# Attention and a leaky-ReLU layer pair in one kernel: the block loads of the later queries issued by GpSimd instead of SyncE

## The chip, the cores and the metric

The kernel runs on one core of a Trainium2 chip. The core has five engines that each work through their own instructions in order: TensorE (PE in the profile; PEld is its weight load), VectorE (DVE), ScalarE (ACT), GpSimd (POOL) and SyncE (SP, which here only issues transfers). They wait for one another through semaphores. Transfers between the main memory and the on-chip memory are carried out by 16 DMA engines, whichever engine issued them. The metric is the time of one execution in microseconds (us); lower is better.

## The reference, cut to what matters

```python
# q, k, v: (4, 8, 768, 64)   lam: (8,)   w_in: (512, 2048)   w_out: (2048, 512)
for b in range(nb):                       # 12 blocks of 64 positions
    sl = slice(b * block, (b + 1) * block)
    qb, kb, vb = (q[:, :, sl], k[:, :, sl], v[:, :, sl])
    intra = np.einsum('bhic,bhjc->bhij', qb, kb) * Dmask[None]
    intra = np.einsum('bhij,bhjd->bhid', intra, vb)
    inter = np.einsum('bhid,bhde->bhie', qb * lam_pow[None], kv_state)
    out[:, :, sl] = intra + inter
    kb_dec = kb * rev_pow[None]
    kv_state = lam_block[None, :, None, None] * kv_state + np.einsum('bhsd,bhse->bhde', kb_dec, vb)
# out, as x: (3072, 512)
h = x @ w_in
g = np.maximum(0.01 * h, h)
return g @ w_out
```

A decayed linear attention over blocks of 64 positions, with a state per head that each block hands to the next, and then two matrix products with a leaky ReLU between them. All data are float32.

## The kernel before, in words

**Stages.** The 3072 tokens are cut into 24 chunks of 128 (two blocks of 64; 6 chunks for each of the 4 batches). Chunk by chunk the attention is computed (`round_of`), 4 chunks make a group of 512 tokens, and each group goes through the first matrix product against 8 blocks of `w_in` (`up`, TensorE at L709). Every float32 factor is split into three parts (`xh`, `xl`, `xm` and `wh`, `wl`, `wm`), so each product is three passes. The results `g` (buffers `gs`) are stored in main memory (L738, L744) or first combined into sums for a Strassen scheme and then stored (`sums`, L766 and L774). While that goes on, the weights `w_out` are loaded (L578), converted by ScalarE and VectorE (L596 to L603) and stored again (L663). The second product (L834) begins at about 330 us and reads the stored blocks back (L808).

**A round of attention.** For chunk c the scores are computed from the transposed keys `kT` and queries `qT` (64x64 matrix instructions, L321), VectorE applies the decay (L460) and adds to the state (L467), GpSimd scales the state by its decay (L470), the keys (L427) and the queries (L431, which makes `qsT`). `kT`, `qT` and `qsT` have two buffers each.

**Where the transposed queries come from.** Up to chunk 9, chunks are loaded straight (L346) and transposed on TensorE (L411). From chunk `DV = 10` on, the loads deliver the queries and keys cut in blocks of 32x32 and VectorE transposes those (`turn`, L391). `load_subs` (L382) issues these block loads for a run of up to 3 chunks at once: 16 transfers for the keys and 16 for the queries of each run, runs being chunks 10 to 11, 12 to 14, 15 to 17, 18 to 20 and 21 to 23. One transfer fills 32 partitions with 8 (first run) or 12 pieces of 32 numbers each, 32 or 48 KB. The queries land in `kqv_f[1]` (a part of `att`), for the run 12 to 14 in `w32` and `lows`; the keys in the `raws` buffers. Each run's queries must land in a buffer that the run before has been transposed out of. `turn(c)` waits for the loads of its run; what it writes, `kT` and `qT` of chunk c, is read by the scores of that chunk and by L431.

**What sets the order.** No scheduler of the language decides: `Plan` collects every step with its engine, an estimated length, what it reads and writes, and a rank, simulates the engines, and emits the instructions of all engines in the order it found. Steps on `"DMA"` are issued on SyncE; `move` adds such a step, with a length for the issue and a `slack` by which the plan moves back the time at which a consumer may count on the data. `Plan.LAG` holds the delay from an engine's end to its consumer's start (0.12 for POOL, 3.5 for DMA). A changed length or engine of one step therefore changes the order on every engine.

**SyncE's queue.** It holds all transfers of the kernel but one: block loads, chunk loads, weight loads, stores of `g`, of the sums and of the weights. It works in order, so a transfer that waits or takes long holds those behind it.

Of the kernel before, what the change touches and what calls it, by code (L numbers as in the profile page):

```python
# [31 lines left out]
def _bc(ap, idx, n):  # L32
    a = [list(x) for x in ap.ap]
    return bass.AP(ap.tensor, ap.offset, a[:idx] + [[0, n]] + a[idx:])


class Plan:
# [23 lines left out]
    def add(self, eng, us, fn, reads=(), writes=(), rank=0.0):  # L61

        n, deps = len(self.ops), set()
        for k in reads:
            w, r = self.last.setdefault(k, [None, []])
            if w is not None:
                deps.add(w)
            r.append(n)
        for k in writes:
            w, r = self.last.setdefault(k, [None, []])  # L70
            if w is not None:
                deps.add(w)
            deps.update(r)
            self.last[k] = [n, []]
        deps.discard(n)
        ways = {eng: us} if isinstance(eng, str) else dict(zip(eng, us))
        if self.slack:
            self.more[n] = self.slack
        if self.chain is not None:
            self.chains[self.chain].append(n)  # L80
        self.ops.append((ways, fn, deps, (self.rank + rank, n), set(writes)))
# [81 lines left out]
def kernel(  # L163
# [10 lines left out]
    nc = tc.nc  # L174
# [19 lines left out]
    SLACK, GSLACK = 4.0, 2.0  # L194
# [5 lines left out]
    LEAD = 8.0  # L200
    WSLACK = 5.0
    DV = 10
    RUNS = {10: (-8.0, 0.8), 12: (4.0, 0.0)}
    C4 = P // 4
    HALF = (slice(0, D), slice(D, 2 * D))
# [72 lines left out]
    plan = Plan()  # L278
    plan.idle, plan.spare, plan.warm = busy, "b10", 1.3 + 0.22 * WARM
    add = plan.add  # L280
    steady = False

    def length(us, issue=0.5):

        return issue if steady else us

    def move(us, fn, reads, writes, issue=0.5, rank=0.0, slack=SLACK):

        plan.slack = slack if steady else EARLY_SLACK
        if steady and not rank:  # L290
            rank = FIRST
        add("DMA", length(us, issue), fn, reads, writes, rank=rank)
        plan.slack = 0.0


    def factors_k():
        for i in range(2):
            nc.vector.tensor_copy(lam_h[:, i * HP:(i + 1) * HP], lam_b[:, i::2])
        nc.vector.tensor_tensor(eye, ident[:, 0:C2], ident[:, C2:C], op=ALU.add)
        for hi in range(2):  # L300
            for hp in range(HP):
                nc.vector.tensor_tensor_scan(decay[:, hi, hp, :], _bc(lam_h[:, 2 * hp + hi], 1, C2), eye, 0.0,
                                             op0=ALU.mult, op1=ALU.add)
# [9 lines left out]
    lam_c = pow_q[:, :, C2 - 1]  # L313
    plan.rank = -1.0
    add("DVE", 1.95, factors_k, [], ["fk", "sc"])
    add("DVE", 1.25, factors_q, [], ["fq"])
    ENG = {"ACT": nc.scalar, "DVE": nc.vector, "POOL": nc.gpsimd}
# [16 lines left out]
    def of(c):  # L334
        return c // NCB, c % NCB, c % 2
# [3 lines left out]
    def load_kq(c):  # L339
        b, n, i = of(c)  # L340
        for src, x, nm in ((k, 0, "k"), (q, 1, "q")):
            y, dst = src[b, :, n * C:(n + 1) * C, :], kqv[x][i]

            def go(y=y, dst=dst):
                for z in range(2):
                    nc.sync.dma_start(out=dst[:, z * HP:(z + 1) * HP, :], in_=y[z::2].rearrange("h p d -> p h d"))  # L346
            if nm == "k" or c < DV:
                move(1.15, go, [], [f"{nm}{i}"], issue=1.0)

    def run(c):  # L350

        lo = max(DV, c - c % TURN)
        return lo, c - c % TURN + TURN - lo

    def subs(first, n):


        n = n * C
        def rows(x, lo, hi):
            return x[:, :(hi - lo) * n].rearrange("p (y t) -> p y t", t=n), lo, hi  # L360
        ks = [(*rows(raw[-2], 0, 2), [f"raw{NRAW - 2}"]), (*rows(raw[-1], 2, 4), [f"raw{NRAW - 1}"])]
        qs = [(*rows(kqv_f[1], 0, HP), ["q0", "q1"])]

        if first == DV:
            ks = [(*rows(raw[0], 0, HP), ["raw0"])]
        elif first < DV + TURN:
            qs = [(*rows(w32f, 0, 2), ["w320", "w321"])] + [
                (*rows(lows[i].bitcast(F32), 2 + i, 3 + i), [f"low{i}"]) for i in range(2)]
        return ks, qs

    def load_subs(c):
        b, n, i = of(c)
        count = run(c)[1]
        for nm, src, pieces in zip("kq", (k, q), subs(c, count)):
            for sub, lo, hi, keys in pieces:
                add("POOL", 0.0, lambda: None, [], keys, rank=-30.0)
                for y in range(lo, hi):
                    for a in range(4):
                        h = y // 2 + (2 * y + a // 2) % HP * 2
                        z = src[b, h, n * C:(n + count) * C, a % 2 * C4:(a % 2 + 1) * C4]  # L380
                        o = sub[a * C4:(a + 1) * C4, y - lo, :]
                        move(0.55, lambda o=o, z=z: nc.sync.dma_start(  # L382
                                out=o.rearrange("j (m i) -> j m i", i=C4), in_=z.rearrange("(m j) i -> j m i", j=C4)),
                            keys, [f"{nm}s{y}{a}"], issue=SUBL, rank=RUNS.get(c, (4.0, 0.4))[0] + RUNS.get(c, (4.0, 0.4))[1] * (4 * y + a))

# [13 lines left out]
    def transposes(c):  # L399
# [9 lines left out]
        def go(src, at):  # L409
            for y in range(HP):  # L410
                nc.tensor.transpose(out=at[y], in_=src[:, 2 * y:2 * y + 2, :].rearrange("p a d -> p (a d)"), identity=ident)  # L411

        if c < DV:
            add("PE", 0.44, lambda: go(tk, at), [f"k{i}"], [key])
            add("PE", 0.44, lambda: go(tq, [pt[:, y, :] for y in range(HP)]), [f"q{i}"], ["pt"])

        def copies():
            kT = kTs[i]
            into = kT if c < GC else kT.rearrange("p (t a) x -> p t (a x)", t=2)
            src = z if c < GC else z.rearrange("p t a x -> p t (a x)")  # L420
            if c < DV:
                add("ACT", 0.6, lambda: nc.scalar.copy(into, src), [key], [f"kT{i}"])
# [115 lines left out]
    def round_of(c):  # L538

        after = []  # L540
        if c + 2 < NCH:
            load_kq(c + 2)
        plan.begin(c)

        if c < 2 * GC:
            after.append(transposes(c + 2))
        after.insert(0, outputs(c, lambda: after.append(scores(c + 1)) if c + 1 < NCH else None))
        if 2 * GC <= c < NCH - 2:
            after.append(transposes(c + 2))
        plan.end()  # L550
        for x in after:
            x()
        if DV < c + 3 < NCH:
            turn(c + 3)
        if DV + TURN < c + 4 < NCH and (c + 4) % TURN == 0:
            load_subs(c + 4)
        if c + 2 < NCH:
            load_v(c + 2)
# [413 lines left out]
    for n, x in enumerate(seq):  # L972
        plan.rank = float(n)
        steady = begin <= n and x[0] in ("r", "up", "wo")
        if x[0] in "abr":
            {"a": alone, "b": begun, "r": round_of}[x[0]](x[1])
        elif x[0] == "ls":
            load_subs(DV)
            turn(DV)
        elif x[0] == "lt":  # L980
            load_subs(sum(run(DV)))
        elif x[0] == "wi":
            w_in(x[1])
        elif x[0] == "up":
            up(*x[1:])
        elif x[0] == "wo":
            w_out(*x[1:])
        elif x[0] == "wp":
            if not freed:
                add("DVE", 0.0, lambda: None, [], ["psc", "po", "X0", "X1", "Z0", "Z1"])  # L990
                freed = True
            w_out_parts(x[1])
        elif x[0] == "ws":
            if x[1] == 0:
                add("DVE", 0.0, free_attention, [], ATT + [f"e{z}{p}" for z in "hlm" for p in range(NS)])
            w_sums(x[1])
        elif x[0] == "fr":
            add("ACT", 0.0, free_raws, [], [f"raw{i}" for i in range(NRAW)] + ["rh4", "rl4", "rm4", "zr"])
        elif x[0] == "s":
            strassen(*x[1:], LEAD)  # L1000
        elif x[0] == "n":
            plain(*x[1:], LEAD)
        elif x[0] == "copy":
            copy_banks(*x[1:])
        elif x[0] == "add":
            add_banks(*x[1:])
        else:
            plain(*x[1:4], LEAD, True, x[4])
# [31 lines left out]
```

## Time and profile before

| | |
|---|---|
| median of 3 runs | 611.8 us (609.57, 611.80, 612.82) |
| profiled execution, its own time | 613.76 us |
| its span, first to last instruction | 611.9 us |
| granted TensorE clock, mean | 0.99 |
| GpSimd busy, 72 to 275 us | 45.40 of 203 us, 48 instructions |
| VectorE busy, 140 to 280 us | 64.34 of 140 us |
| DMA engines busy, 140 to 280 us | 0.87 |
| packets under 512 bytes, 140 to 280 us | 58413 of 74066 |
| L382, block loads of keys / queries | 80 / 80 issues on SyncE, 94.2 to 272.2 us / 72.8 to 274.6 us |
| one such issue, least / median / most | keys 312 / 490 / 1921 ns; queries into `att` 419 / 474 / 1827 ns |
| from issue to landing, queries, median | 3.1 us (the 48 of 48 KB into `att`) |

The profile is that of one execution. "Busy" counts the time in which an engine carries out instructions; issuing a transfer does not count. A wait is put down to the event that came last: "[2.37 <-ACT b L727]" behind an instruction says that its engine stood 2.37 us before it, until ScalarE's instruction of line 727 had written a tile `b`. "SPq" is SyncE's queue: its rows show when a transfer was issued and how long the issue took, not when the data landed. The granted clock is the share of full speed that TensorE was given.

### The profile page before, as it was taken

The numbers are of one execution on the slowest core, as the hardware profiler recorded it, in microseconds if no ns is written. First come the engines' busy times: TensorE is split into PE (matmuls) and PEld (weight loads), VectorE is DVE, ScalarE is ACT, GpSimd is POOL, SyncE is SP. The second block draws the span as 40 slices with busy tenths as digits, with TensorE's granted clock in tenths as the row PEclk, the third lists the DMA queues.
The fourth block names the chain that finished last, engine by engine and source line by source line (L and its number), as shares of the span: only waits on it lengthen the run. The fifth ranks groups of instructions, "written<-read, shape, count | busy, mean of one in ns | idle before, by whom it ended". The sixth has DMA issues, their size and how long they took to land.

```text
span 611.9 us, 13190 instructions
## 1 busy us (share of the span) xinstructions
PE 591.6 (97%) x5340; PEld 488.7 (80%) x5340; DVE 387.4 (63%) x534; ACT 290.4 (47%) x458; POOL 85.9 (14%) x90
## 2 busy tenths in 40 slices
PE   7899999999989999999999999999999999999994
PEld 6688888888868877888888888888887888878883
DVE  4899764335436327426589849975688695778831
ACT  4678974445545545565576743432334223251300
POOL 1564422114214003203100000000000000000000
PEclk9899999999989999999999999999999999999998
DMA  9899776767889887999889735436465465474433
GB/s 217 212 261 254 228 193 145 171 151 204 196 218 264 216 220 218 235 235 260 265 256 333 233 113 197 170 123 185 139 182 195 152 193 176 155 225 140 158 80 69
DMA packets 190188, 119.88 MB, mean 196 GB/s; under 512 B 128944, under 2 KB 168112, under 8 KB 190128
## 3 DMA queue, kind: packets, MB, share of 16 engines
q1 hardware_dynamic: 189984, 119.05, 68.8%
q8 instruction: 42, 0.69, 0.5%
q14 instruction: 18, 0.15, 0.1%
q10 hardware_dynamic: 144, 0.00, 0.0%
HBM read 79.17 MB, written 39.85 MB: 194 GB/s over the span
## 4 chain that ended last, share of the span: by engine, by line
PE 84%; DMA 4%; SPq 4%; DVE 3%; ACT 2%; issue 1%; DVEq 0%; ACTq 0%
PE b L709 40%; PE b L834 11%; PE psc L834 11%; PE po L834 10%; PE po L321 4%; PE psc L321 4%; PE pt L834 4%; SPq L382 2%; SPq L911 2%; DMA att<-in_v_dram 1%; DMA raws<-in_moe_w_out_dram 1%; DVE xl L814 1%; PE pt L411 1%; DMA xm<-g 1%; DMA raws<-g 1%
## 5 line engine op out<-in xcount | busy, mean ns | idle before, releaser
L709 PE MATMUL b<-xm,wm 128*128 128x512 f32 (+2 forms) x392 | 103.9, 392 | 2.4 <-ACT b L727 2.4
L709 PE MATMUL b<-xh,wh 128*128 128x512 f32 (+2 forms) x392 | 103.5, 387 | 2.3 <-ACT gs L732 1.5
L709 PE MATMUL b<-xl,wl 128*128 128x512 f32 (+2 forms) x392 | 104.4, 390 | 0.0
L709 PEld LDWEIGHTS b<-xh,wh 128*128 128x128 f32 x392 | 72.8, 188 | 18.2 <-ACT gs L732 2.4
L811 ACT ACTIVATE xh<-xm 128x1024 fp32r<-128x1024 f32 x45 | 47.7, 1060 | 81.8 <-DMA xm<-g 50.9
L709 PEld LDWEIGHTS b<-xm,wm 128*128 128x128 f32 x392 | 71.4, 188 | 17.8 <-ACT b L727 3.2
L709 PEld LDWEIGHTS b<-xl,wl 128*128 128x128 f32 x392 | 72.8, 188 | 15.1 <-DVE wl L614 0.3
L732 ACT ACTIVATE gs<-b 128x512 f32<-128x512 f32 (+2 forms) x97 | 56.9, 591 | 50.6 <-PE b L709 37.4
L727 ACT ACTIVATE b<-b 128x512 f32<-128x512 f32 (+2 forms) x97 | 56.1, 581 | 52.2 <-PE b L709 52.0
L814 DVE SCALAR_TENSOR_TENSOR xl<-xm,xh 128x1024 fp32r<-128x1024 f32 x45 | 54.8, 1217 | 28.3 <-ACT xh L811 22.1
L818 DVE SCALAR_TENSOR_TENSOR xm<-xl,xh 128x1024 fp32r<-128x1024 f32 x48 | 58.7, 1225 | 3.5
L470 POOL TENSOR_TENSOR att<-att 128x256 f32<-128x256 f32 x40 | 34.1, 853 | 53.9 <-DVE att L467 53.9
L602 DVE TENSOR_SCALAR w<-w 128x512 int32<-128x512 int32 x32 | 17.6, 550 | 36.9 <-ACT w L596 36.8
L431 POOL TENSOR_TENSOR att<-att 128x512 f32<-128x512 f32 (+1 forms) x20 | 25.2, 1261 | 102.0 <-DVE att L391 53.9
L460 DVE TENSOR_TENSOR att<-psc,att 128x512 f32<-128x512 f32 x24 | 16.5, 689 | 31.3 <-PE psc L321 31.2
L321 PEld LDWEIGHTS po<-att 64*64 64x64 f32 x1472 | 28.3, 140 | 9.1 <-issue 6.0
L321 PE MATMUL po<-att 64*64 64x64 f32 x1472 | 34.1, 228 | 0.6 <-ACT att L499 0.3
L427 POOL TENSOR_TENSOR att<-att 128x512 f32<-128x512 f32 (+1 forms) x23 | 26.7, 1161 | 53.7 <-DMA att<-in_k_dram 35.9
L603 DVE CUSTOM_DVE_ANT_0 w<-w,lows 128x1024 uint16<-128x1024 uint16 x32 | 26.3, 821 | 12.6 <-ACT lows L600 11.4
L834 PE MATMUL b<-xl,wl 128*128 128x512 f32 (+1 forms) x86 | 33.0, 384 | 0.0
L834 PE MATMUL b<-xm,wm 128*128 128x512 f32 (+1 forms) x86 | 33.0, 384 | 0.0
L834 PE MATMUL b<-xh,wh 128*128 128x512 f32 (+1 forms) x86 | 33.0, 384 | 0.0
(149 smaller groups left out, 1011.2 us busy)
## 6 DMA issues: line engine op xcount, KB each, us to landing
g<-gs SPq DMA_DIRECT2D x31, 512.0 KB, 4.1
xm<-g SPq DMA_DIRECT2D x25, 512.0 KB, 4.7
xm<-b SPq DMA_DIRECT2D x23, 512.0 KB, 3.8
raws<-in_moe_w_in_dram SPq DMA_DIRECT2D x16, 512.0 KB, 5.5
raws<-in_moe_w_out_dram SPq DMA_DIRECT2D x16, 512.0 KB, 5.0
b<-gs SPq DMA_DIRECT2D x16, 512.0 KB, 3.7
att<-in_k_dram SPq DMA_DIRECT2D x48, 128.0 KB, 4.0
att<-in_v_dram SPq DMA_DIRECT2D x24, 256.0 KB, 4.5
```

The lines of the kernel that those rows point to most:

```text
L321: nc.tensor.matmul(dst[HALF[cols]], lhsT=lhsT[HALF[rows]], rhs=rhs[HALF[rows]], start=start, stop=True, skip_group_check=True)
L427: lambda e="POOL": ENG[e].tensor_tensor(kr[nr], kr[nr], _bc(pow_k, 3, D)[nr], op=ALU.mult), ["fk"], [f"k{i}"])
L431: add(eng, us, lambda: e.tensor_tensor(o, x, _bc(pow_q, 2, 2)[:, :, m, :], op=ALU.mult), ["fq", dep], [f"qsT{i}"])
L470: add("POOL", 0.7, lambda new=new, j=j: nc.gpsimd.tensor_tensor(state[(j + 1) % 4], new, _bc(lam_c, 2, D), op=ALU.mult), [f"st{j % 4}", "f ...
L603: add("DVE", 1.0, lambda: nc.vector.tensor_tensor(d, d, low, op=ALU.add), [kl], [key])
L709: nc.tensor.matmul(dst, lhsT=w[z][:, kk * 2 * P + f * P:kk * 2 * P + (f + 1) * P], rhs=x[z][:, kk, toks], start=start and kk == 0, stop=kk ...
L727: add("ACT", ns, lambda b=b: nc.scalar.activation(out=b, in_=b, func=AF.Copy, bias=0.0, scale=S + 1.0), [], [kb], rank=-1.5)
L732: add("ACT", t, lambda o=o, x=s_: nc.scalar.activation(out=o, in_=x, func=AF.Prelu, bias=0.0, scale=(1.0 + 1.0 / S) / (WS * U), alpha=0.01 ...
L811: nc.scalar.activation(out=ring[j][0], in_=g(), func=AF.Copy, bias=0.0, scale=NEAR)
L814: nc.vector.scalar_tensor_tensor(ring[j][1], g(), 1.0, ring[j][0].bitcast(F32), op0=ALU.mult, op1=ALU.subtract)
L818: nc.vector.scalar_tensor_tensor(m, l.bitcast(F32), -S, h.bitcast(F32), op0=ALU.mult, op1=ALU.add)
L834: nc.tensor.matmul(dst, lhsT=lhs(z), rhs=ring[j][z][:, col:col + n], start=first and z == 0, stop=z == 2, skip_group_check=True)
```

## The change

The 80 query loads of `load_subs` are issued by GpSimd (`nc.gpsimd.dma_start`), the 80 key loads still by SyncE. In the plan they become steps on the engine `"POOL"`, each with a length of `QSL = 1.0` us instead of an issue of `SUBL = 0.75` (0.55 early on) on `"DMA"`, and with a slack of 3.5 - 0.12 + 2.0 = 5.38 us before a consumer may count on the data. The sources, the destinations, the sizes and the count of the transfers stay.

```diff
     DV = 10
+    QSL = 1.0
     RUNS = {10: (-8.0, 0.8), 12: (4.0, 0.0)}
...
+    def carry(us, fn, reads, writes, issue=0.0, rank=0.0):
+
+        plan.slack = plan.LAG["DMA"] - plan.LAG["POOL"] + GSLACK
+        add("POOL", us, fn, reads, writes, rank=rank)
+        plan.slack = 0.0
+
...
-                        move(0.55, lambda o=o, z=z: nc.sync.dma_start(
+                        (move if nm == "k" else carry)(0.55 if nm == "k" else QSL, lambda o=o, z=z, e=nc.sync if nm == "k" else nc.gpsimd: e.dma_start(
                                 out=o.rearrange("j (m i) -> j m i", i=C4), in_=z.rearrange("(m j) i -> j m i", j=C4)),
                             keys, [f"{nm}s{y}{a}"], issue=SUBL, rank=RUNS.get(c, (4.0, 0.4))[0] + RUNS.get(c, (4.0, 0.4))[1] * (4 * y + a))
```

The plan lays out all engines anew. On GpSimd the query loads stand between the scalings: for the run 10 to 11 in pieces of 2, 2, 9 and 3 loads, for the run 12 to 14 as 1, 1, 1 and then 13 in a row, and for the later runs mostly as one to four at a time with pieces of 6, 7 and 8 among them, around L427, L431 and L470. On SyncE the key loads of a run follow one another, where key and query loads alternated before. On TensorE the counts of all matrix instructions stay; the order of some groups of L709 and the place of some rounds among them shift. The new lines move the line numbers behind line 302 by 7: L382 is L389 in the changed kernel.

## The prediction

> **What bounds the kernel now.** I read the page first, its busy line and its chain of work that ended last.
>
> ```profile
> PE 591.6 (97%) x5340; PEld 488.7 (80%) x5340; DVE 387.4 (63%) x534; ACT 290.4 (47%) x458; POOL 85.9 (14%) x90
> ...
> PE 84%; DMA 4%; SPq 4%; DVE 3%; ACT 2%; issue 1%; DVEq 0%; ACTq 0%
> ```
>
> TensorE is busy for 97% of the span, so only its pauses, 20.3 us (611.9 - 591.6), can be won, and only those that the moved loads cause. L382, the line of those loads, issues from 72.8 to 274.6 us. The busy time by stretch shows where TensorE pauses inside that time (columns: TensorE, weight load, VectorE, ScalarE, GpSimd busy, granted clock, DMA share, GB/s):
>
> ```profile
> 160.00:180.00 20.00, 17.63 (x195) 14.30 (x194) 6.20 (x14) 10.37 (x18) 2.69 (x3) 0.98 0.76 183
> 180.00:200.00 20.00, 20.00 (x320) 16.48 (x320) 13.40 (x23) 9.07 (x19) 7.77 (x9) 0.93 0.97 259
> ...
> 220.00:240.00 20.00, 18.46 (x199) 14.65 (x198) 8.91 (x18) 9.88 (x19) 4.26 (x5) 1.00 0.83 244
> ```
>
> Two pauses, 2.37 us and 1.54 us; the other stretches from 40 to 300 us are full. The timeline of TensorE around them:
>
> ```profile
> 178.12 1.20 PE L709 MATMUL b<-xm,wm 128*128 128x512 f32 x4 [2.37 <-ACT b L727]
> 179.15 1.70 PE L709 MATMUL b<-xl,wl 128*128 128x512 f32 x4
> 180.78 1.56 PE L321 MATMUL po<-att 64*64 64x64 f32 x48
> 182.11 1.42 PE L321 MATMUL psc<-att 64*64 64x64 f32 x64
> ...
> 227.97 1.20 PE L709 MATMUL b<-xh,wh 128*128 128x512 f32 x4 [1.37 <-ACT gs L732]
> ```
>
> After the first pause three groups take 1.70, 1.56 and 1.42 us where the same groups elsewhere take 1.07, 0.93 and 1.11: 1.57 us more, with the granted clock at 0.93 in that stretch. Both pauses name ScalarE, so its timeline is next:
>
> ```profile
> 176.25 0.66 ACT L596 ACTIVATE w<-raws 128x512 f32<-128x512 f32 x1 [3.52 <-DMA raws<-in_moe_w_out_dram]
> ...
> 227.31 0.60 ACT L732 ACTIVATE gs<-b 128x512 f32<-128x512 f32 x1 [3.73 <-DMA b<-gs]
> ```
>
> ScalarE stood 3.52 us for a weight load and 3.73 us for a store, with TensorE's bank behind it. What held those two transfers is in SyncE's timeline:
>
> ```profile
> 165.46 0.96 SPq L382 DMA_DIRECT2D att<-in_q_dram  x1
> 166.47 0.82 SPq L382 DMA_DIRECT2D raws<-in_k_dram  x1
> 167.34 0.54 SPq L382 DMA_DIRECT2D att<-in_q_dram  x1
> ...
> 170.56 0.45 SPq L578 DMA_DIRECT2D raws<-in_moe_w_out_dram  x1
> ...
> 218.65 0.47 SPq L382 DMA_DIRECT2D att<-in_q_dram  x1
> 219.16 0.47 SPq L382 DMA_DIRECT2D raws<-in_k_dram  x1
> 219.68 0.47 SPq L382 DMA_DIRECT2D att<-in_q_dram  x1
> ...
> 221.74 0.39 SPq L774 DMA_DIRECT2D b<-gs  x1
> ```
>
> The weight load's buffer was free at 163.22 (end of ScalarE's L600, 162.44 + 0.78) and its issue came at 170.56. The store's data were ready at 217.98 (end of VectorE's L766) and its issue came at 221.74. SyncE did block loads meanwhile.
>
> **The change, part by part.** *Removed from SyncE:* 80 issues (16 of 32x8x32, 64 of 32x12x32) at a median of 0.474 us: 38 us of its queue. For the first pause, two of them (0.96 + 0.54 us) stand directly before the weight load, and six more (0.47 to 1.58 us, 4.4 together) delay the queue from 155 us on. In the new order the stores of L774, the loads of L396 and L346 and then L578 follow one another with no query load between them; by their rows (0.42 + 0.45 + 0.42 + 1.96) that is 3.3 us after the k load that ends at 164.34 now. Even with no earlier start, L578 issues near 168; with the six gone ahead of it, I put it near 166, some 4.5 us sooner. ScalarE's wait was 3.52. So the 2.37 us and the 1.57 us behind it go. For the second pause, five query loads between 214.8 and 219.7 (0.62 + 0.56 + 0.47 + 0.47 + 0.47 = 2.6 us) go, the store starts up to 2.6 us sooner, and the 1.54 us pause goes. Together 2.37 + 1.57 + 1.54 = 5.5 us.
>
> *Added to GpSimd:* 80 issues, X us each. The trace has no GpSimd transfer, so X is bounded. Below: SyncE's 0.47 us for the same transfer. Above: GpSimd must itself write out 384 pieces (32 x 12), for reading and for writing. Its L470 takes 0.62 us for 256 elements a lane and L427 1.06 us for 512: 1.72 ns an element and 0.18 us before. 384 steps once are 0.84 us, twice 1.50 us; drawn out as L470 is on the page (853 ns mean over 616 least, 1.38) 2.1 us. I take 1.2, between the once and the twice, since most L470 after 180 us run at 0.62 to 0.83.
>
> *What hides it:* GpSimd is busy 7.68, 5.98 and 6.26 us in the three stretches in which SyncE now issues the queries of chunks 15 to 17, 18 to 20 and 21 to 23 (34.33, 37.34 and 35.41 us long). 16 issues fit beside it up to X = 26.65/16 = 1.67, 1.96 and 1.82. At 1.2 they take 19.2 us, so the queries land sooner than now. The earlier 32 issues lie where no pause is near.
>
> *What queues behind them:* GpSimd works in order, so L427 (scaled keys), L431 (scaled queries) and L470 (decayed state) stand behind query loads, and these behind L470's wait for VectorE. The new order puts one to three loads between two L470 in most rounds, with runs of 8 to 13 ahead of an L427. The cover: a round's last L470 ends 4.75 us before TensorE's next round (187.35 to 192.10), 6.5 us (197.83 to 204.33), at the narrowest 2.0 (120.28 to 122.31); L427 ends 13 us before its use (192.09 to 205.1). The planner reckons 1.0 a load, so at 1.2 a run of 13 is 2.6 us late against that. Gone the cover, each us late is a us of TensorE and 0.66 us of slower clock (1.57/2.37).
>
> *The planner* lays all queues anew, matrix groups included; TensorE's count does not change. I charge one new pause of the size of the second, 1.5 us. Bounds: nothing, and both pauses back, 5.5.
>
> The sum on the profiled execution (613.76 us, span 611.9): 613.76 - 5.5 + 1.5 = 609.8. It ran 1.96 us above the median of the three runs, so on the median 607.8.
>
> L470 lasts from 616 to 1610 ns, stretched where VectorE is busy beside it (46% of the time from 140 to 280 us). The Trainium skill (SBUF — State Buffer, section "SBUF: two separate sides") goes further against this change: a VectorE operation in a two-port mode shuts GpSimd out of the port through which it writes descriptors, a 620 ns transfer then taking about 3100. An estimate by that page alone, 80 loads at 3.1 us, gives 248 us on GpSimd where 203 us are to hand, so slower by over 45 us; no run here shows it yet.
>
> **The rivals.** *GpSimd too slow (slower).* If X is 2.1, the last query of each run comes 16 x (2.1 - 1.67) = 6.9, 2.2 and 4.5 us later than now. Margins now, from the end of the query's transpose (L391) to the scores: under 1.1 us (181.85 to 182.9), 1.8 and 2.6. TensorE then stands 5.8 + 0.4 + 1.9 = 8.1 us, with the clock 13.4. Less the 5.5 recovered: 611.8 + 7.9 = 619.7. The two balance near X = 1.95 (16 x 0.28 - 1.1 = 3.4 us of pause, 5.6 with the clock), which decides it. For it: no row bounds X firmly, and the scarce margin. Against: GpSimd is busy 14%, and the element rate above. A long tail belongs to it: all 80 stretched like the worst L470 (2.6 times 1.5 = 3.9 us) would be about 100 us late in the three runs.
>
> *The transfers are the limit, not their issue (no change).* In the stretch 180 to 200 the DMA engines are busy 0.97, and some SyncE issues take 1.0 to 2.0 us, which looks like a queue held back by full engines. The same bytes from another queue would then land no sooner, the weight load included: 611.8. Against it: the share is 0.76 in 160 to 180, where the first pause is.
>
> The Trainium skill (DMA: Bandwidth & Descriptors, section "Issuing engines are not separate DMA queues") sides with that rival: all issuers share the same 16 engines and only the sequencer's time is saved. Here that time is what stands on the chain, so the trace bears out the first half only.
>
> **How the numbers follow.** Forecast 0.48, its own range 605.5 to 610; no change 0.16; GpSimd too slow 0.36. What this kernel's measurement can tell from no change is about 0.5%, 3.1 us (the three runs span 609.57 to 612.82). Of the forecast's 0.48, 0.43 lies below 608.7 and 0.05 above; the second case is all within; the third is all slower. So faster 0.43, same 0.21, slower 0.36. The range runs from 604.5 (5.5 gained, and 1.8 more of TensorE's other pauses) to 623 (X near 2.2); about 0.04 lies below and 0.12 above.
>
> **What would show it.** Right: no pause over 1 us on TensorE from 160 to 240; ScalarE's wait at L596 for the weight load under 1 us; GpSimd's issues near 1.2 us; SyncE's query issues gone from the chain. Wrong: issues near 2 us with L431 or the scores waiting for the query load or for GpSimd, or the weight load still landing late with SyncE free, or new pauses where the planner moved a store.

## The result, and the profile after

| | before | after |
|---|---|---|
| median, 19 runs each | 612.43 us (609.57 to 616.61) | 608.32 us (606.33 to 611.22) |
| ratio of the times | | 0.9935, 95% interval 0.9920 to 0.9951 |
| profiled execution, its span | 613.76 us, 611.9 us | 607.87 us, 606.1 us |

The changed kernel is faster by 4.1 us (612.43 - 608.32), 0.65%. The two profiled executions differ by 5.9 us; that is more than the medians do, since the one of before ran above its median, so the sizes below are held against the medians. The medians below are those of each kernel's usual runs; one run with 8 additions and one with the keys on GpSimd too took 1191 us and are left out.

The busy line, two of the DMA queues (packets, bytes in MB, share of the engines' time) and the chain of work that ended last, from the page of after:

```profile
PE 588.6 (97%) x5340; PEld 486.5 (80%) x5340; DVE 391.5 (65%) x533; ACT 291.2 (48%) x459; POOL 132.7 (22%) x170
...
q1 hardware_dynamic: 160032, 115.37, 65.7%
q0 software_dynamic: 2560, 3.68, 2.7%
...
PE 91%; DVE 4%; DMA 1%; SPq 1%; issue 1%; ACT 1%; POOL 0%; DVEq 0%; POOLq 0%; ACTq 0%
```

GpSimd has 80 instructions and 46.8 us more: unlike SyncE's, its issues are counted as busy time. On the chain SyncE's queue went from 4% to 1% and the transfers from 4% to 1%; TensorE took their place (84% to 91%).

The busy time by stretch, for the same three stretches as before (TensorE, weight load, VectorE, ScalarE, GpSimd, granted clock, DMA share, GB/s):

```profile
160.00:180.00 20.00, 20.00 (x326) 16.54 (x325) 12.91 (x24) 11.04 (x20) 7.82 (x10) 1.00 0.86 239
180.00:200.00 20.00, 20.00 (x248) 16.43 (x250) 10.47 (x19) 11.72 (x21) 14.69 (x22) 1.00 0.99 247
...
220.00:240.00 20.00, 20.00 (x192) 16.58 (x191) 9.59 (x17) 11.59 (x21) 12.32 (x18) 1.00 0.99 243
```

Both pauses are gone and the clock behind the first is back from 0.93 to 1.00. From 40 to 300 us TensorE pauses three times, 0.37, 0.56 and 0.28 us, 1.21 together, none at the old places. Why the first of the two old pauses is gone stands in SyncE's timeline:

```profile
160.73 0.39 SPq L781 DMA_DIRECT2D b<-gs  x1
161.37 0.39 SPq L781 DMA_DIRECT2D b<-raws  x1
161.85 0.89 SPq L403 DMA_DIRECT2D att<-in_v_dram  x1
162.84 2.11 SPq L353 DMA_DIRECT2D att<-in_k_dram  x2
165.04 0.95 SPq L585 DMA_DIRECT2D raws<-in_moe_w_out_dram  x1
```

The weight load (L578 before, L585 now) is issued at 165.04 instead of 170.56, with no query load ahead of it. The transfer itself is not the difference: from issue to landing the 16 weight loads take 5.0 us before and 4.7 after (medians). ScalarE's timeline shows the consumer without a bracket, so without a wait, where it stood 3.52 us before:

```profile
171.85 0.65 ACT L603 ACTIVATE w<-raws 128x512 f32<-128x512 f32 x1
```

And the price of the moved issues, by the rows of line L389 on GpSimd (ns least/median/most, first and last start in us):

```profile
L389 POOL DMA_DIRECT2D att<-in_q_dram x64: 582/615/769, 71.3 to 234.7; - x64
L389 POOL DMA_DIRECT2D w<-in_q_dram x8: 615/628/642, 111.7 to 121.9; - x8
L389 POOL DMA_DIRECT2D lows<-in_q_dram x8: 615/616/617, 122.5 to 126.7; - x8
```

GpSimd takes 0.62 us for a load, half of the 1.2 that the forecast reckoned with.

### The profile page after: what moved, and what is told of

It reads as the page before. It is cut to its first block, busy times and chain, and to the rows that moved or that the text cites. A ratio compares the mean times of both kernels' runs of the same rounds, so it can differ in the third digit from the quotient of the medians.

```text
span 606.1 us, 13233 instructions
## 1 busy us (share of the span) xinstructions
PE 588.6 (97%) x5340; PEld 486.5 (80%) x5340; DVE 391.5 (65%) x533; ACT 291.2 (48%) x459; POOL 132.7 (22%) x170
## 3 DMA queue, kind: packets, MB, share of 16 engines
q1 hardware_dynamic: 160032, 115.37, 65.7%
q0 software_dynamic: 2560, 3.68, 2.7%
## 4 chain that ended last, share of the span: by engine, by line
PE 91%; DVE 4%; DMA 1%; SPq 1%; issue 1%; ACT 1%; POOL 0%; DVEq 0%; POOLq 0%; ACTq 0%
PE b L716 44%; PE b L841 12%; PE po L841 11%; PE psc L841 11%; PE pt L841 4%; PE po L328 4%; PE psc L328 4%; SPq L918 1%; DMA raws<-g 1%; PE pt L418 1%; DMA att<-in_k_dram 1%; PE po L418 1%; DVE xm L825 0%; DVE xl L821 0%; DVE att L467 0%
## 5 line engine op out<-in xcount | busy, mean ns | idle before, releaser
L389 POOL DMA_DIRECT2D att<-in_q_dram x64 | 39.5, 623 | 3.9 <-DVE att L398 1.7
L609 DVE TENSOR_SCALAR w<-w 128x512 int32<-128x512 int32 x32 | 19.5, 610 | 26.9 <-ACT w L603 26.9
```

The lines of the kernel that those rows point to most:

```text
L389: (move if nm == "k" else carry)(0.55 if nm == "k" else QSL, lambda o=o, z=z, e=nc.sync if nm == "k" else nc.gpsimd: e.dma_start(out=o.rea ...
```

## The experiments

The ratios are those of the times to the kernel before, with 95% intervals. The theory at the start: taking the query loads off SyncE's queue removed the two pauses, and nothing else matters. Rivals: the new order of all engines did it; or GpSimd's share of the work has a price that the cover hides only just.

**The old order, queries on GpSimd.** In the kernel before, only the issuing engine of the query loads is changed, so the order on TensorE, VectorE and ScalarE stays as it was.

```diff
-    move(0.55, lambda o=o, z=z: nc.sync.dma_start(
+    move(0.55, lambda o=o, z=z, e=nc.sync if nm == "k" else nc.gpsimd: e.dma_start(
```

> The old plan kept (order on TensorE, VectorE and ScalarE as before), only the 80 query loads issued by GpSimd. Theory, SyncE's queue was late: the two pauses of 2.37 and 1.54 us go, ratio to before about 0.993 (-4 us). Rival, the gain came from the planner's new order: 1.000, both pauses still there.

606.91 us, ratio 0.9931 (0.9914 to 0.9947): all of the gain. The busy time by stretch of this run:

```profile
160.00:180.00 20.00, 20.00 (x326) 16.63 (x325) 10.79 (x21) 11.50 (x20) 7.51 (x10) 1.00 0.86 247
...
220.00:240.00 20.00, 20.00 (x310) 16.60 (x309) 13.90 (x27) 11.57 (x22) 8.15 (x11) 1.00 0.73 209
```

TensorE is full in both stretches; from 140 to 300 us it is busy 159.72 of 160. Since the order is that of before, the second pause can be followed too. The store behind it, in SyncE's timeline, and ScalarE's wait for it:

```profile
213.72 0.39 SPq L774 DMA_DIRECT2D b<-gs  x1
```

```profile
219.76 0.60 ACT L732 ACTIVATE gs<-b 128x512 f32<-128x512 f32 x1 [0.57 <-DMA b<-gs]
```

Its data were ready at 213.01 (the end of VectorE's L766), so its issue came 0.71 us after them, where it came 3.76 us after them before (217.98 to 221.74). ScalarE stood 0.57 us for it instead of 3.73. The plan's own knowledge of the move (`carry`, `QSL`, the slack) adds nothing that can be measured.

**The new order, queries on SyncE.** The changed kernel with all loads of L389 back on SyncE.

```diff
-    (move if nm == "k" else carry)(..., e=nc.sync if nm == "k" else nc.gpsimd: e.dma_start(
+    (move if nm == "k" else carry)(..., e=nc.sync: e.dma_start(
```

> The new plan kept, but the 80 query loads issued by SyncE again. Theory (queue): the gain is gone, ratio 1.000 or above, up to 1.015 since the plan no longer reckons with these issues on SyncE; TensorE waits over 1 us between 140 and 300 us. Rival (order): 0.9935 as in the changed kernel.

619.35 us, ratio 1.0141 (1.0114 to 1.0167). ScalarE's and then TensorE's timeline of this run:

```profile
176.91 0.66 ACT L603 ACTIVATE w<-raws 128x512 f32<-128x512 f32 x1 [4.43 <-DMA raws<-in_moe_w_out_dram]
```

```profile
178.78 1.20 PE L716 MATMUL b<-xm,wm 128*128 128x512 f32 x4 [3.29 <-ACT b L734]
```

The first pause is back, longer than before (3.29 us, 2.37 then), with ScalarE at the same wait. The new order with the loads left on SyncE is slower than before, so the order is not what gained. (It was laid out for a SyncE without these loads, so it does not price an order by itself; that the old order has all of the gain is the firmer half of the argument.)

**Which runs of queries.** In the old order, only the 48 loads of chunks 15 to 23 on GpSimd, or only the 32 of chunks 10 to 14.

```diff
+    move(0.55, lambda ..., e=nc.gpsimd if nm == "q" and c >= 15 else nc.sync: ...   # the late ones
+    move(0.55, lambda ..., e=nc.gpsimd if nm == "q" and c < 15 else nc.sync: ...    # the early ones
```

> The old plan kept, query loads of chunks 15 to 23 (48) by GpSimd, those of chunks 10 to 14 (32) by SyncE. Theory: both pauses lie between 160 and 232 us, among the loads of the later runs, so nearly the whole gain: ratio about 0.994. Rival (all SyncE issues count alike, 48 of 80): 0.996. Rival (order): 1.000.

> The old plan kept, only the query loads of chunks 10 to 14 (32) by GpSimd. Theory: no pause lies there, so no gain, ratio 1.000. Rival (all issues count alike): 0.997.

The late ones: 607.74 us, ratio 0.9938 (0.9919 to 0.9958), so all of it within the interval. The early ones: 612.49, ratio 1.0020 (1.0003 to 1.0037), none. With the early ones alone, TensorE's timeline still has the first pause, if a shorter one:

```profile
176.70 1.20 PE L709 MATMUL b<-xm,wm 128*128 128x512 f32 x4 [1.42 <-ACT b L727]
177.73 1.07 PE L709 MATMUL b<-xl,wl 128*128 128x512 f32 x4
```

Other pauses came with it: from 40 to 300 us they add up to 4.59 us, against 3.91 before. The gain comes from the loads that lie around the two pauses. The second row has its ordinary 1.07 us: behind these 1.42 us of standing the clock stayed at 1.00, while it fell behind the 2.37 us of before.

**A dearer load, by additions.** To find how much GpSimd may spend on a load, the changed kernel does 2, 4 or 8 small additions on GpSimd ahead of each query load, into a tile that nobody reads.

```diff
+    drag = sb([P, 48], "drag")
...
+    for _ in range(2):          # 4, 8
+        nc.gpsimd.tensor_tensor(drag, ident[:, 0:48], ident[:, 0:48], op=ALU.add)
```

> The changed kernel with 2 small GpSimd additions (128x48) ahead of each query load, about 0.26 us each by L470's row, so that a load costs GpSimd some 1.15 us, near the 1.2 of the prediction. Theory, GpSimd has cover: ratio 0.993 to 0.996, the cover hides nearly all. Rival, the gain hangs on loads as short as 0.62 us: 1.000 or slower.

> 4 such additions ahead of each query load: some 1.65 us a load. The prediction has the three later runs of loads keep pace up to 1.67, so ratio below 1.000, about 0.995 to 1.000; the balance of gain and loss was put at 1.95. Rival (works in order, L470 and L427 late at once): 1.005 to 1.015.

> 8 such additions ahead of each query load: some 2.7 us a load. By the prediction's working the queries come 16, 12 and 14 us late in the three runs, about 55 us slower than before, ratio 1.09, TensorE standing for GpSimd (L431, L427 or the scores). Rival (there is far more cover than was reckoned): below 1.02.

| additions a load | us a load on GpSimd | time, us | ratio |
|---|---|---|---|
| none (after) | 0.62 | 608.32 | 0.9935 (0.9920 to 0.9951) |
| 2 | 1.20 | 611.36 | 0.9997 (0.9976 to 1.0017) |
| 4 | 1.89 | 659.79 | 1.0799 (1.0773 to 1.0824) |
| 8 | 3.26 | 765.99 | 1.2546 (1.2513 to 1.2578) |

None of the three forecasts held; with 2 additions its rival came about, with 4 and 8 the loss was far larger than either said. At 1.2 the gain is gone, and at 1.89, where the forecast's sum of busy times still saw a gain, the kernel is 8% slower. GpSimd's timeline with 4 additions, at the end of the run of 13 loads (L441 is L427 of before, the scaled keys), and TensorE's beside it:

```profile
152.60 0.62 POOL L396 DMA_DIRECT2D lows<-in_q_dram  x1
153.22 1.30 POOL L382 TENSOR_TENSOR drag<-att 128x48 f32<-128x48 f32 x4
154.48 0.62 POOL L396 DMA_DIRECT2D lows<-in_q_dram  x1
155.11 2.08 POOL L441 TENSOR_TENSOR att<-att 128x512 f32<-128x512 f32 x2
```

```profile
156.23 1.98 PE L329 MATMUL psc<-att 64*64 64x64 f32 x64 [6.79 <-POOL att L441]
```

TensorE stands 6.79 us for the scaled keys, which stand behind the 13 loads, and then runs slowly (1.98 us for a group that takes 1.11 in after). Over 140 to 300 us:

```profile
140.00:300.00 160.00, 127.57 (x1535) 104.38 (x1533) 56.55 (x115) 64.78 (x117) 129.60 (x315) 0.91 0.68 179
```

TensorE is busy for 127.57 of 160 us at a clock of 0.91; GpSimd is busy for 129.60, still not all the time. So it is not only GpSimd's busy time that decides, but also what waits behind a run of loads. Waits for L441 are 13.0 us of TensorE's standing in this run. Late queries are in it too: VectorE's transposes stood 51.4 us in four waits for query loads into `att` (0.8 in after). How the 48 us of loss divide between the two is open. With 8 additions TensorE stands 48.8 us in two waits for L441.

**The same, with the plan told.** Two additions, and the plan given a length of 1.25 us a load.

```diff
-    QSL = 1.0
+    QSL = 1.25
```

> The kernel with 2 small additions ahead of each query load (1.20 us a load, ratio 0.9997 with the plan at 1.0), the plan now told 1.25. Theory (the gain was lost because the plan laid GpSimd's work for 1.0 a load): 0.994 to 0.997. Rival (in-order work on GpSimd costs it, whatever the plan says, or the additions slow VectorE): 0.999 or above.

612.85 us, ratio 1.0025 (1.0005 to 1.0045). The order made for the dearer load wins nothing back, as the rival said. Its profile has one pause of 3.20 us, again behind ScalarE's wait for a store (`b<-gs`):

```profile
214.52 1.20 PE L723 MATMUL b<-xh,wh 128*128 128x512 f32 x4 [3.20 <-ACT gs L746]
215.56 1.08 PE L723 MATMUL b<-xl,wl 128*128 128x512 f32 x4
```

This pause is longer than the 2.37 us of before, and yet the groups behind it keep their ordinary 1.07 to 1.08 us and the clock stays at 1.00.

**A dearer load, by a second load.** Additions read the on-chip memory and may slow VectorE as well. So the same time on GpSimd was spent in another way: a small load of 32 pieces into an unused tile ahead of each query load.

```diff
+    nc.gpsimd.dma_start(out=drag[a * C4:(a + 1) * C4, 0:C4], in_=z[0:C4, :])
```

> The changed kernel with a second, small load (32x32) by GpSimd ahead of each query load: some 1.2 us a query load, without the additions' reads of the shared memory. Theory (GpSimd's time for a load is what matters): as with 2 additions, 0.998 to 1.002. Rival (the additions took the gain by slowing VectorE): 0.993 to 0.996.

608.05 us, ratio 0.9953 (0.9936 to 0.9971), with GpSimd's rows:

```profile
L381 POOL DMA_DIRECT2D drag<-in_q_dram x80: 517/517/877, 72.2 to 241.4; - x80
...
L395 POOL DMA_DIRECT2D att<-in_q_dram x64: 594/627/954, 72.9 to 242.0; - x64
```

0.517 + 0.627 = 1.14 us a query, nearly as long as with two additions (1.20), and the run of 13 loads ends as late (136.87 us, 136.62 with additions, 129.39 in after). But the gain stays, so GpSimd's time for a load is not all that matters, as the theory of this run had it. One thing that differs is VectorE. One of its groups, the same work in all three kernels, from 60 to 300 us (count, busy us, mean ns, wait before), first with additions, then with the second load, then in after:

```profile
L532 DVE SCALAR_TENSOR_TENSOR xm<-xl,xh 128x512 fp32r<-128x512 f32 x18 | 17.7, 982 | 0.7
```

```profile
L531 DVE SCALAR_TENSOR_TENSOR xm<-xl,xh 128x512 fp32r<-128x512 f32 x18 | 15.9, 882 | 0.7
```

```profile
L525 DVE SCALAR_TENSOR_TENSOR xm<-xl,xh 128x512 fp32r<-128x512 f32 x18 | 15.7, 873 | 0.7
```

982 ns against 882 and 873: GpSimd's additions stretch VectorE by 12% in this group, GpSimd's loads by 1%. The Trainium skill (SBUF — State Buffer, section "Who interferes with whom") has this distinction: a VectorE operation with two inputs in the on-chip memory contends with a GpSimd operation that reads that memory, but not with one that only writes there. The three rows agree. Yet VectorE also waits longer for queries with additions (its transposes of `att` stood 24.4 us for them in that profile, 8.6 with the second load, 0.8 in after), and the profiled execution with additions (609.96 us) lies below its median, so the runs don't say how the 3.3 us between the two kernels (611.36 - 608.05) divide between a slower VectorE and later queries.

**Keys on GpSimd too, and the true price in the plan.**

```diff
-    (move if nm == "k" else carry)(..., e=nc.sync if nm == "k" else nc.gpsimd: e.dma_start(
+    carry(QSL, lambda o=o, z=z, e=nc.gpsimd: e.dma_start(      # keys too
```

```diff
-    QSL = 1.0
+    QSL = 0.6
```

> Both the key and the query loads (160) by GpSimd, planned at 0.6 us each, which is what the trace of the changed kernel shows for one (0.62). Theory (only the two pauses were to be won, and they are gone): 0.990 to 0.996, no more than 1.5 us from the changed kernel. Rival (each issue taken off SyncE gains): 0.988. Rival (GpSimd too full or its transfers land too late, 160 x 0.62 = 99 us more): above 0.998.

> The changed kernel with the plan told 0.6 us a load, what the trace shows (0.62), in place of 1.0. Theory (the gain is the two pauses, already gone; the order adds nothing): 0.991 to 0.996. Rival (a plan with the true price wins more): below 0.991.

Keys too: 607.93 us, ratio 0.9957 (0.9940 to 0.9973). The price of 0.6: 608.18, ratio 0.9948 (0.9930 to 0.9966). Neither can be told from after. That fits the theory of both runs: with 1.21 us of pauses left from 40 to 300 us there is little more to win by emptying SyncE's queue.

**The other side of the queue: the weight loads on GpSimd.** In the old order, the 16 loads of L578, one of which was the late one, are issued by GpSimd; all block loads stay on SyncE.

```diff
-    nc.sync.dma_start(out=r64, in_=moe_w_out[...])
+    nc.gpsimd.dma_start(out=r64, in_=moe_w_out[...])
```

> The old plan kept, all block loads on SyncE, but the 16 weight loads of L578 issued by GpSimd. Theory: the first pause came from that load's late issue, so it goes (2.37 us and the slow clock), the second pause, of a store held by block loads, stays: 0.995 to 0.998. Rival (GpSimd, in order, stands at the load's wait for its buffer, and L470 and L427 behind it): 1.005 or above.

610.60 us, ratio 0.9991 (0.9974 to 1.0009): not told from no change, so neither the theory's range nor the rival's. The table of waits of this run (total us, times, longest us) has on top of GpSimd's rows:

```profile
POOL raws L578 <- ACT lows L600: 59.5, 10, 11.3
```

These 16 loads wait for their buffer, and on GpSimd what is queued behind them waits with them: it stood 59.5 us for that alone. In its profile both old pauses are gone, the second against the expectation. Its store was still issued 3.04 us after its data were ready (214.51 to 217.55, block loads ahead of it), but ScalarE stood only 0.44 us for it, since the store let its buffer go within 3.4 us of its issue, where before that took 5.6. So a late issue made that pause together with a slow transfer, not by itself (in the old order with the queries on GpSimd it took 6.0, the issue was in time, and there was no pause). A new pause of 1.14 us, which the trace puts down to a transpose on VectorE (L391), came at 179.74. Its profiled execution (609.78 us) lies below its median, and what its other runs lost is not settled.

## Why the prediction was right, and where it was not

**The bound.** Right. TensorE's pauses behind late transfers were what could be won, and both went as soon as the late query loads left SyncE (the runs in the old order with all and with the late ones). The weight load's issue had been late by SyncE's queue: the buffer was free, and its issue moved from 170.56 to 165.04 (forecast: near 166).

**The size of the gain.** The two pauses, 3.91 us, are gone as forecast. The slow clock behind the first, 1.57 us, is gone from the profile too. The charge for new pauses, 1.5 us, stands against 1.21 left, at other places. So 5.5 - 1.5 = 4.0 was forecast and the medians show 4.1. That they meet so closely is in part luck. The charge was a guess, taken from the size of the second pause. And the term for the clock holds for the profiled execution alone: its mean granted clock is 0.990, while 20 other executions of the kernel before lie from 0.992 to 0.997 with a median of 0.996, and the median of after's 19 is 0.996 too. By these clocks, that term was hardly there to be won in a usual execution. The pauses of the profiles give 3.91 - 1.21 = 2.7 us; the rest of the 4.1 is not shown, since those other executions left no trace. Nor does each us of standing cost 0.66 us of slower clock, as the forecast charged on the cover's side: the pause of 3.20 us cost none. The larger difference of the profiled executions (5.9 us) has a part that does not come from the moved loads: before's had a clock of 0.91 from 20 to 40 us, ahead of the first of them, and the four kernels in its order (all queries on GpSimd, the late ones, the early ones, the weights) have 1.00 there.

**The price of an issue.** Mis-sized. X was taken as 1.2, from the time of GpSimd's arithmetic for each element, and measured 0.62. That working is wrong in kind, not only in size: GpSimd's issue hardly follows the pieces. A load of 32 pieces takes 0.517 us and the query loads, with 256 or 384 pieces, 0.582 to 0.616 least. From 32 to 384 that is 0.099 us for 352 pieces, 0.28 ns a piece, on a fixed half microsecond; the forecast had 1.72 ns for each element. The Trainium skill (DMA: Bandwidth & Descriptors, section "Anatomy of one DMA — SWDGE (gpsimd) path") says that many descriptors can be emitted before the added cost shows; these rows agree, as far as 384 pieces. The forecast did not hang on the size: real loads that took GpSimd 1.14 us a query still gave 0.9953.

**The cover.** The step that failed, though the forecast did not depend on it at the measured price: "16 issues fit beside it up to X = 1.67, 1.96 and 1.82", and from it the point of balance "near X = 1.95". At 1.89 us a load the kernel was 8% slower, 48 us, where no loss was expected. The sum set GpSimd's busy time against the length of a run of chunks, as if the loads could be moved freely among the scalings. In fact GpSimd works in order, and the plan had put 13 loads in a row ahead of the scaled keys. These 13 are among "the earlier 32 issues", which the forecast set aside because they "lie where no pause is near"; with 4 additions the first two long stands of TensorE from 40 us on, 4.39 us up to 118.46 and 6.79 us up to 156.23, come in their stretch. The three later runs were mis-sized as well: by the forecast's working a load of 1.89 us makes their queries 16 x (1.89 - 1.67) = 3.5 us, nothing and 1.1 us late, and the transposes stood 9.1, 13.4 and 8.6 us for them. What the forecast said elsewhere, "a run of 13 is 2.6 us late", was the right quantity and was not carried into the point of balance: 13 loads of 1.89 instead of the planned 1.0 are 11.6 us late, and the trace shows 6.79 us of standing there, with a clock of 0.83 over the 20 us around it. The additions weigh on VectorE too, so the exact balance for loads alone lies somewhere above 1.14 us and was not found.

**The rivals.** "GpSimd too slow" had a chance of 0.36 and did not come, since X is far below its 2.1; with X drawn out to 1.89 it came, and much harder than its 619.7. "The transfers are the limit" fell: in the two stretches of the old pauses the DMA share rose, from 0.76 to 0.86 and from 0.83 to 0.99, and the pauses went. Full engines were no sign that the weight load was late; the queue ahead of its issue was. The locked port, by which an issue would take some 3.1 us, did not show: the longest of the 80 took 0.769 us, with VectorE busy for 83.5 of the 160 us from 140 to 300. No view here tells which of VectorE's operations ran in a two-port mode, so the lock itself is not tested.

## What to carry to other kernels

Where an engine waits for a transfer, compare the time at which its buffer or data was ready with the time of its issue: if the queue held it, move the many small issues ahead of it that wait for nothing, not the one that waits for its buffer: here the first gained 0.7% and the second nothing that could be measured. A load issued by GpSimd is to be priced by the count of transfers; between 32 and 384 pieces it hardly grew. And the cover on an engine that works in order is read at the longest run of moved instructions and the first work behind it, early runs included, not from its share of busy time.

## What the runs showed of the hardware

- An issue by GpSimd takes 0.517 us for 32 pieces, 0.582 to 0.616 for 256 to 384, and 0.593 (median) for a whole weight block:

```profile
L578 POOL DMA_DIRECT2D raws<-in_moe_w_out_dram x16: 530/593/722, 120.2 to 315.8; - x16
```

- The same loads count as far fewer packets from GpSimd's queue: 2560 for 80 loads, 32 each, where SyncE's queue lost 29952 (189984 - 160032), 374 each. The DMA engines' time for them is about the same, 2.7% of the span on the one and 68.8 - 65.7 = 3.1% on the other. From issue to landing they take 4.1 us (median of the 48 into `att`), 3.1 before.
- What a pause does to TensorE's clock did not follow from its length. One of 1.42 us cost nothing; one of 2.37 us was followed by a stretch of 20 us at 0.93 and one of 3.29 us (new order, queries on SyncE) by one at 0.91; but one of 3.20 us (two additions, told to the plan) was followed by a stretch at 1.00. What decides it is open here.
